# Linear attention and channel mix on one core: key moves on one queue, half of the weight loads behind unit 0's keys, other costs and due times in the plan

## The chip, the core and the metric

The kernel runs on one core of one Trainium2 chip. A core has a matrix engine (TensorE, PE in the profile) with its own sequencer for weight loads (PEld), two engines for elementwise work (VectorE or DVE, ScalarE or ACT), GpSimd (POOL) and SyncE (SP). SP and POOL issue the transfers of this kernel; the transfers themselves run on 16 DMA engines. The metric is the device time of one execution in microseconds, the median of the runs shown.

## The reference

A linear attention with a complex decay, followed by a channel mix. Per batch (4), head (8) and step (768), with a head size of 48:

```python
mag = np.sqrt(a_re * a_re + a_im * a_im)
scale = np.minimum(mag, 0.999) / (mag + 1e-06)
...
for t in range(S):
    new_re = ar * S_re - ai * S_im
    new_im = ar * S_im + ai * S_re
    kv = np.einsum('bhd,bhe->bhde', k[:, :, t], v[:, :, t])
    S_re, S_im = (new_re + kv, new_im)
    y[:, :, t] = np.einsum('bhd,bhde->bhe', q[:, :, t], S_re)
```

The heads are put side by side (x, 384 wide), and then, with x_prev the row before:

```python
xk = mu_k * x + (1.0 - mu_k) * x_prev
xr = mu_r * x + (1.0 - mu_r) * x_prev
k = np.maximum(xk @ w_k, 0.0)
v = k * k @ w_v
r = 1.0 / (1.0 + np.exp(-(xr @ w_r)))
return (r * v)
```

w_k is 384 x 1024, w_v 1024 x 384, w_r 384 x 384; everything is float32 (the weights arrive as 64-bit numbers and are converted on the chip).

## The kernel before

**Tiling.** The 4 x 768 rows are cut into eight units of 384 tokens (two halves per batch, the second one starting from the state of the first). Each unit has three steps:

- `gate(u)` loads a tile `g` of [a_re, a_im, k, q] in three parts of 128 channels (L662) and the values `v` (L671), and computes with ACT and DVE the decay's logarithm and angle, running sums of both, and at the end (`times`, L797, DVE) k and q multiplied by the cosine and by the sine of the angle.
- `attend(u)` is the attention. `stack(h)` moves a head's 48 channels of the cosine part and the 48 of the sine part of `g` into one tile `kq`, 112 rows high (L834, a transfer within the chip). Heads 2 and 5 straddle two parts of `g` and take two transfers for each part, so a unit has 20: heads with 48 rows move 144 KB at once. There are six buffers `kq` for eight heads, so the last two heads wait until the values of the first pairs are done; in unit 0 the last two use free space in `x0`. `scores` (sc, L914) multiplies keys and queries, DVE masks the result (pt, L923), `values` (y, L949 and L955) multiplies it with v and the state, ACT copies y to `ys` (L964), and ten transfers move `ys` into `xt` (L970), which is x with channels on partitions. `advance` carries the state: TensorE turns k (tr, L865), ACT copies it to `kt` (L871), and `up` (L885) multiplies it with v.
- `mix(u)` is the channel mix: differences and sums of x and x_prev on DVE and ACT, the products z (L461) for w_k and w_r, relu and square (L497, L501), the product with w_v (o, L528), and the store. For accuracy each float32 operand is split into a high and a low part (x and its rest, `hhi` and `hlo`), three products in place of one; unit 0 alone uses the whole float32 weights (L456, L525).

The weights come in ten pieces, `raw` (piece 0 of 384 KB, nine of 768 KB). `fetch(i)` loads a piece (`fetched`, L381), `convert(i)` makes float32 of it in three instructions on ACT and DVE (L589 to L599), and `split(i)` makes the high and the low part (L622, L625). Pieces 2 to 9 hold one block of w_k and one of w_v each. `look(i)`, 19 in all, loads a block of the weights once more (tile `again`, L638) and checks its range (DVE L642, ACT L644 and L645).

**What sets the order.** The whole program is a list of operations, each with its engine, its cost in us, what it reads and writes and which buffers it holds. The class `Plan` turns it into an order: each operation gets a due time, backwards from the products of TensorE, whose places come from the table `AT` (for each unit one pair of numbers for `attend` and one for `mix`); then a simulation of the engines starts, whenever an engine is free, the ready operation with the earliest due time. For SP and GP (POOL) it counts an issue time and a shared DMA stream with a START and an ARRIVE time. The instructions are emitted in the order of these simulated starts. So costs and due times change nothing but the order in which each engine's instructions stand (and, for operations that may run on either of two engines, which of them takes it). Between the times when `r` of unit 0's angle and its first hidden product are planned (FILL), an idle TensorE is given small products that nobody reads (`warm`, L1008, fillers).

`op_move` is an operation that either SP or POOL may issue; before the change all moves to kq and xt are of this kind. `op_dma` is one of SP, `op_dma_gp` one of POOL. Each engine works its instructions strictly in its own order, so a transfer that waits holds back those that stand behind it on the same engine.

## Time and profile before

| | us |
|---|---|
| median of three runs | 482.07 |
| lowest and highest | 478.08, 485.91 |
| the profiled execution, whole | 481.24 |
| its span in the trace | 479.5 |
| mean granted clock of TensorE | 0.958 |

The span is what the profile's page and its views divide by; 1.74 us of the profiled execution lie around it. What the page says of the transfers by number and queue, with the KB of each and the median us from issue to landing:

```profile
g<-in_gat SPq DMA_DIRECT2D x18, 768.0 KB, 6.0
kq<-g POOLq DMA_DIRECT2D x51, 144.0 KB, 5.5
again<-in_w_all SPq DMA_DIRECT2D x19, 384.0 KB, 4.1
kq<-g SPq DMA_DIRECT2D x43, 144.0 KB, 5.5
out_t<-zr SPq DMA_DIRECT2D x24, 192.0 KB, 2.0
```

The 144 KB moves of keys are split about evenly between the two queues. A wait in the views below is idle time of an engine and the event that ended it; it costs time only where that engine sets the end at that moment.

### The profile page before, as it was taken

The page shows a single profiled execution, that of the slowest core. Times are in us where ns is not written, and L with a number is a line of the kernel's source. Part 1 is how long each engine was busy: PE and PEld are TensorE (multiplying, and loading weights), DVE is VectorE, ACT ScalarE, POOL GpSimd, SP SyncE. Part 2 cuts the span into 40 slices and gives each one's busy share as a digit, 9 for nine tenths or more (in the row PEclk, how much of TensorE's full clock was granted, in tenths as well). Part 3 has the DMA queues.
Part 4 walks back from the last instruction along what each step waited for, and adds up shares of the span by engine and source line. Part 5 has one row for each costly group of instructions (what it writes and reads, how often), then busy time and mean ns, then how long its engine had stood idle before and what let it go on. Part 6 is the DMA issues. An engine that isn't in the chain of part 4 may idle for free.

```text
span 479.5 us, 9560 instructions
## 1 busy us (share of the span) xinstructions
PE 402.3 (84%) x3625; PEld 361.6 (75%) x3625; DVE 331.3 (69%) x523; ACT 346.1 (72%) x611; POOL 78.8 (16%) x179
## 2 busy tenths in 40 slices
PE   1015999999579997999799988999699979998994
PEld 1004985676368987989688977899588979898993
DVE  6794779477678996668777886696648985154322
ACT  5995558965769896979778896987686975335440
POOL 6332120211302120102110130202020020300000
PEclk9999799999889998999999998999689998999998
DMA  8999370708926671485947473597353182300101
GB/s 297 412 354 223 132 220 17 133 17 262 200 83 176 205 154 28 109 276 190 161 116 265 141 134 83 128 326 130 85 158 109 34 181 83 75 26 1 51 0 57
DMA packets 26053, 69.91 MB, mean 146 GB/s; under 512 B 5696, under 2 KB 10432, under 8 KB 26000
## 3 DMA queue, kind: packets, MB, share of 16 engines
q1 hardware_dynamic: 19232, 46.37, 33.9%
q0 software_dynamic: 6768, 22.86, 17.9%
q8 instruction: 30, 0.49, 0.4%
q14 instruction: 23, 0.19, 0.1%
HBM read 40.90 MB, written 4.72 MB: 95 GB/s over the span
## 4 chain that ended last, share of the span: by engine, by line
PE 36%; DMA 20%; issue 14%; ACT 13%; DVE 12%; POOL 3%; SPq 1%; POOLq 0%; DVEq 0%; ACTq 0%
PE z L461 11%; DMA kq<-g 11%; PE o L528 9%; PE sc L914 4%; DMA again<-in_w_all 4%; PE up L885 3%; DMA raw<-in_w_all 2%; DVE g L797 2%; DMA xt<-ys 2%; PE y L949 2%; PE o L525 2%; DVE ph L764 2%; PE y L955 2%; PE tr L865 1%; ACT r L303 1%
## 5 line engine op out<-in xcount | busy, mean ns | idle before, releaser
L461 PE MATMUL z<-x,w 128*128 128x384 f32 x693 | 132.0, 340 | 0.1
L461 PEld LDWEIGHTS z<-x,w 128*128 128x128 f32 x693 | 120.8, 188 | 2.2 <-issue 0.7
L528 PE MATMUL o<-hhi,w 128*128 128x384 f32 x336 | 89.0, 346 | 0.0
L834 POOL DMA_DIRECT2D kq<-g x77 | 39.0, 509 | 227.8 <-PE y L955 150.8
L914 PE MATMUL sc<-kq 112*64 112x64 f32 (+1 forms) x744 | 52.2, 283 | 25.2 <-DMA kq<-g 20.5
L914 PEld LDWEIGHTS sc<-kq 112*64 112x64 f32 x744 | 44.7, 159 | 35.0 <-issue 25.0
L528 PEld LDWEIGHTS o<-hhi,w 128*128 128x128 f32 x336 | 60.2, 190 | 2.1 <-issue 1.5
L528 PE MATMUL o<-hlo,w 128*128 128x384 f32 x168 | 57.3, 341 | 1.4 <-DVE hlo L509 1.4
L497 ACT ACTIVATE r<-z 128x384 f32<-128x384 f32 x64 | 31.0, 484 | 28.0 <-PE z L461 26.6
L865 PE MATMUL tr<-ident,g 128*128 128x128 f32 x120 | 22.0, 315 | 31.2 <-DVE g L797 31.2
L923 DVE TENSOR_TENSOR pt<-sc,masks 128x512 int32<-128x512 int32 x48 | 31.6, 684 | 23.8 <-PE sc L914 23.7
L797 DVE TENSOR_TENSOR g<-g,r 128x768 f32<-128x768 f32 x48 | 43.8, 951 | 4.2 <-ACT r L303 4.1
L865 PEld LDWEIGHTS tr<-ident,g 128*128 128x128 f32 x120 | 16.0, 160 | 34.7 <-DVE g L797 32.2
L970 POOL DMA_DIRECT2D xt<-ys x40 | 21.8, 546 | 91.5 <-ACT ys L964 84.6
L871 ACT COPY kt<-tr 128x384 f32<-128x384 f32 x40 | 18.1, 473 | 21.7 <-PE tr L865 21.5
L501 ACT ACTIVATE h<-r 128x384 f32<-128x384 f32 x64 | 33.0, 521 | 0.8
L528 PEld LDWEIGHTS o<-hlo,w 128*128 128x128 f32 x168 | 31.9, 190 | 1.7 <-DVE hlo L509 1.7
L885 PE MATMUL up<-v,kt 128*48 128x48 f32 (+1 forms) x640 | 25.5, 234 | 9.1 <-ACT kt L871 8.4
L885 PEld LDWEIGHTS up<-v,kt 128*48 128x48 f32 (+1 forms) x640 | 23.4, 145 | 12.2 <-ACT kt L871 11.2
L509 DVE TENSOR_TENSOR hlo<-h,hhi 128x384 fp32r<-128x384 f32 x56 | 30.9, 556 | 1.2
L319 DVE CAST hhi<-h 128x384 fp32r<-128x384 f32 x31 | 11.1, 357 | 29.0 <-PE o L528 17.3
L303 ACT ACTIVATE sq<-m 128x1152 f32<-128x1152 f32 (+2 forms) x27 | 27.7, 1049 | 3.6 <-DVE m L745 2.7
(91 smaller groups left out, 711.7 us busy)
## 6 DMA issues: line engine op xcount, KB each, us to landing
g<-in_gat SPq DMA_DIRECT2D x18, 768.0 KB, 6.0
kq<-g POOLq DMA_DIRECT2D x51, 144.0 KB, 5.5
again<-in_w_all SPq DMA_DIRECT2D x19, 384.0 KB, 4.1
raw<-in_w_all POOLq DMA_DIRECT2D x9, 768.0 KB, 10.8
kq<-g SPq DMA_DIRECT2D x43, 144.0 KB, 5.5
v<-in_vt SPq DMA_DIRECT2D x21, 288.0 KB, 5.1
out_t<-zr SPq DMA_DIRECT2D x24, 192.0 KB, 2.0
g<-in_gat SPq DMA_DIRECT2D x6, 384.0 KB, 4.7
```

Source lines behind the costliest of these rows:

```text
L303: nc.scalar.activation(out=out, in_=in_, func=func, **kw)
L461: nc.tensor.matmul(z, lhsT=wt[s[0]][:, part, s[1]], rhs=r[which][:, ct], start=n == 0, stop=n == 3 * NT - 1)
L497: nc.scalar.activation(out=t["r", j], in_=t["f", j], func=AF.Relu)
L501: nc.scalar.activation(out=t["h", j], in_=t["r", j], func=AF.Square)
L509: nc.vector.tensor_tensor(out=t["lo", j], in0=t["h", j], in1=t["hi", j].bitcast(F32), op=ALU.subtract)
L528: nc.tensor.matmul(tiles["o", mt], lhsT=wt[W_V + 2 * j][:, part, ts(mt, P)], rhs=r, start=j == 0 and n == 0, stop=j == NJ - 1 and n == 2)
L797: nc.vector.tensor_tensor(out=g[:, ct, 2 * i:2 * i + 2], in0=g[:, ct, 2:4], in1=t["r"][:, ct, 1 - i:2 - i].to_broadcast([P, 2, U]), op=ALU ...
L834: queue.dma_start(out=kq[h][i * HR + o:i * HR + o + n], in_=G[u][s, ct, 2 * i:2 * i + 2])
L865: nc.tensor.transpose(out=t["tr", c, part][:, ct * P:(ct + 1) * P], in_=G[u][:, ct, 2 * part, c * P:(c + 1) * P], identity=ident)
L885: nc.tensor.matmul(t["up", c][rows, h * D:(h + 1) * D], lhsT=both[:, cols], rhs=V[u][c][:, h * D:(h + 1) * D], start=True, stop=True)
L914: nc.tensor.matmul(sc[rows, i, cols], lhsT=kq[2 * p + j][:, 0, c * P + late * Q:][:, :Q], rhs=q if j else q[:, ::-1], start=True, stop=True)
L923: nc.vector.tensor_tensor(out=pts[k, c].bitcast(I32), in0=both, in1=masks.unsqueeze(1).to_broadcast([P, 2, 2, P]), op=ALU.bitwise_and)
```

## The change

- All moves to `kq` are issued by SP. The moves from `ys` to `xt` are also SP's, except in unit 0, where either engine may take them.
- Weight pieces 5 to 9 are loaded by SP, and only after all of unit 0's last products of the gate (its sine part, `kqs`) are there. Pieces 0 to 4 stay with POOL and no longer wait for a part of unit 0's gate.
- In the plan: another table `AT`; ARRIVE 1.3 for 0.9; a move is counted with 220 in place of 380 KB per ms; ACT and DVE instructions have 0.02 us more; the mask of the scores costs less; and the rule that a large transfer starts only when the stream is free now goes by a mark on each operation (`bulk`) instead of by its cost. Moves within the chip and the first two units' gate loads carry no such mark.

No instruction's work changes, only its place, and for the moves and half of the pieces the engine that issues them; the number of fillers, which the plan's idle times set, goes from 40 to 69. The lines of the changed kernel are those of before less one up to line 567, and one more from line 1008 on.

```diff
-AT = ((0.51, 1.23), (0.86, 1.42), (2.31, 2.4), (2.62, 3.27), (2.24, 2.87), (3.17, 4.12), (2.83, 3.65), (4.13, 5.17),
+AT = ((0.42, 0.67), (2.23, 4.26), (0.93, 2.49), (2.73, 3.06), (2.24, 2.87), (3.78, 4.38), (2.83, 3.48), (4.03, 5.22),
...
-FETCH_AT = 0
+FETCHED = 5
...
-    START, ARRIVE = 1.15, 0.9
-    BULK = 0.4
+    START, ARRIVE = 1.15, 1.3
...
-            if o["engine"] in self.QUEUE and o["cost"] > self.BULK and dma > t + self.START:
+            if o["bulk"] and dma > t + self.START:
                 return False
...
-        plan[0].op("ACT", 0.09 + n / 1200, f, **kw)
+        plan[0].op("ACT", 0.11 + n / 1200, f, **kw)
...
-        plan[0].op("DVE", 0.08 + n / (960 * rate), f, **kw)
+        plan[0].op("DVE", 0.1 + n / (960 * rate), f, **kw)
...
-        plan[0].op("SP", n / 380, f, **kw)
+        plan[0].op("SP", n / 380, f, **{"bulk": True, **kw})
...
-        plan[0].op("SP", n / 380, lambda e: f(nc.sync if e == "SP" else nc.gpsimd), other={"GP": n / 380}, **kw)
+        plan[0].op("SP", n / 220, lambda e: f(nc.sync if e == "SP" else nc.gpsimd), other={"GP": n / 220}, **kw)
...
-                raws[i] = fetched(keep, s, nc.gpsimd, tag=f"w{i}")[0]
-            op_dma_gp(393 * n, f, writes=[("raw", i)], reads=[("in", 0, FETCH_AT, 2)])
+                raws[i] = fetched(keep, s, nc.sync if i >= FETCHED else nc.gpsimd, tag=f"w{i}")[0]
+            late = i >= FETCHED
+            (op_dma if late else op_dma_gp)(393 * n, f, writes=[("raw", i)], reads=[("kqs", 0, ct) for ct in range(NT)] * late, bulk=late)
...
-                    uses=[g_slot[u]])
+                    uses=[g_slot[u]], bulk=u >= FIRST_LOAD)
...
-                        queue.dma_start(
+                        nc.sync.dma_start(
                             out=kq[h][i * HR + o:i * HR + o + n], in_=G[u][s, ct, 2 * i:2 * i + 2])
-                    op_move(n * 3.07, f, reads=[("kqs" if i else "kqc", u, r0 // P)], writes=[("st", u, h, i, r0)],
+                    plan[0].op("SP", n * 3.07 / 220, f, reads=[("kqs" if i else "kqc", u, r0 // P)], writes=[("st", u, h, i, r0)],
                            uses=[kq_slot[h], g_slot[u]])
...
-                op_dve(4 * P + 60, f1, reads=[("sc", u, k, c)], writes=[("pt", u, k, c)], uses=[sp, pt_slot[k, c]])
+                op_dve(4 * P, f1, reads=[("sc", u, k, c)], writes=[("pt", u, k, c)], uses=[sp, pt_slot[k, c]])
...
-                    op_move((src.stop - src.start) * 1.54, f, reads=[("ys", u, p), ("X0", u)], writes=[("Xp", u, i, dst.start)],
+                    k = (src.stop - src.start) * 1.54
+                    (op_move if u == 0 else lambda k, f, **kw: plan[0].op("SP", k / 220, lambda: f(nc.sync), **kw))(k, f, reads=[("ys", u, p), ("X0", u)], writes=[("Xp", u, i, dst.start)],
                            uses=[sy, x_slot[u]])
```

How it moves instructions shows in three places. The rows give line, operation, output<-input (with buffer numbers where names would read alike), shape, and a count.

SP at the start of the program, behind the loads of unit 0's gate (g_136): the moves of its keys. Before, seven of the moves into kq stand here with those into x0, the rest on POOL, and behind them comes the load of unit 2's gate (g_418):

```order
L834 DMA kq0_97<-g_136 48x768 x2
L834 DMA kq2_99<-g_136 48x768
L834 DMA kq4_101<-g_136 32x768
L834 DMA kq4_101<-g_136 16x768
L834 DMA kq2_99<-g_136 48x768
L834 DMA x0_132<-g_136 48x768
L834 DMA kq5_102<-g_136 48x768
L834 DMA x0_132<-g_136 16x768
L834 DMA x0_132<-g_136 32x768
L662 DMA g_418<-in_gat 128x1536 x2
```

After the change, from the third head on (six rows of kq0 to kq3 stand ahead of these):

```order
L834 DMA kq4_101<-g_136 32x768
L834 DMA kq2_99<-g_136 48x768
L834 DMA kq3_100<-g_136 48x768
L834 DMA kq4_101<-g_136 32x768
L834 DMA kq4_101<-g_136 16x768 x2
L834 DMA kq5_102<-g_136 48x768 x2
L834 DMA x0_132<-g_136 48x768 x2
L834 DMA x0_132<-g_136 16x768 x2
L834 DMA x0_132<-g_136 32x768 x2
L380 DMA raw_392<-in_w_all 128x6144
L380 DMA raw_413<-in_w_all 128x6144
```

All of unit 0's moves stand on SP, and two weight pieces follow them directly. POOL, which has the pieces, shows it from the other side. Before, with unit 1's gate g_150:

```order
L662 DMA g_150<-in_gat 128x768
L381 DMA raw_214<-in_w_all 128x6144
L381 DMA raw_223<-in_w_all 128x6144
L381 DMA raw_232<-in_w_all 128x6144
L834 DMA kq1_98<-g_136 48x768 x2
L381 DMA raw_249<-in_w_all 128x6144
L381 DMA raw_258<-in_w_all 128x3072
L834 DMA kq3_100<-g_136 48x768
```

After, with unit 1's gate g_140:

```order
L662 DMA g_140<-in_gat 128x768 x6
L671 DMA v_154<-in_vt 128x576
L671 DMA v_159<-in_vt 128x576
L671 DMA v_162<-in_vt 128x576
L380 DMA raw_165<-in_w_all 128x6144
L380 DMA raw_168<-in_w_all 128x6144
L380 DMA raw_173<-in_w_all 128x3072
L380 DMA raw_175<-in_w_all 128x6144
L380 DMA raw_179<-in_w_all 128x6144
L970 DMA xt_156<-ys_447 48x384
```

The last five pieces have left POOL, the first five stand behind the whole of unit 1's gate, and no keys stand among them.

TensorE where unit 4's first scores stand (unit 2's mix lies around them), before:

```order
L461 MATMUL z<-x,w 128x384 x9
L528 MATMUL o<-hhi,w 128x384 x2
L528 MATMUL o<-hlo,w 128x384
L528 MATMUL o<-hhi,w 128x384 x2
L528 MATMUL o<-hlo,w 128x384
L528 MATMUL o<-hhi,w 128x384 x2
L528 MATMUL o<-hlo,w 128x384
L865 MATMUL tr<-ident,g 128x128 x6
L914 MATMUL sc<-kq_97 64x128
```

After (three more products o and then the first score follow these rows):

```order
L460 MATMUL z<-x,w 128x384 x18
L865 MATMUL tr<-ident,g 128x128 x3
L527 MATMUL o<-hhi,w 128x384 x2
L527 MATMUL o<-hlo,w 128x384
L527 MATMUL o<-hhi,w 128x384 x2
L527 MATMUL o<-hlo,w 128x384
L527 MATMUL o<-hhi,w 128x384 x2
L527 MATMUL o<-hlo,w 128x384
L865 MATMUL tr<-ident,g 128x128 x3
L527 MATMUL o<-hhi,w 128x384 x2
L527 MATMUL o<-hlo,w 128x384
```

Between the first turn of the keys and the first score there are now 18 products o; before, there was none.

ACT in unit 6, around the copies to kt (kt_3451 before), before:

```order
L644 ACTIVATE again_3374<-again_3374,consts_82 128x384
L440 CAST x_3419<-xm_3242 128x384
L440 CAST x_3419<-xm_3391 128x384
L479 COPY zr_3423<-z_3397 128x384
L645 ACTIVATE again_3374,stat_92<-again_3374,consts_82 128x384
L440 CAST x_3344<-xm_3425 128x384
L871 COPY kt_3451<-tr_3428 128x8x48
L871 COPY kt_3451<-tr_3434 128x8x48
```

After (kt_3456 and kt_3518 are its first two chunks):

```order
L439 CAST x_3324<-xm_3432 128x384
L871 COPY kt_3456<-tr_3435 128x8x48
L871 COPY kt_3456<-tr_3441 128x8x48
L296 ACT_TABLE_LOAD
L302 ACTIVATE m_3305<-m_3305,consts_82 128x1152
L439 CAST x_3415<-xm_3492 128x384
L439 CAST x_3324<-xm_3503 128x384
L871 COPY kt_3518<-tr_3505 128x8x48
L871 COPY kt_3518<-tr_3511 128x8x48
L302 ACTIVATE ph_3306,stat_92<-m_3305 128x1152
L644 ACTIVATE again_3426<-again_3426,consts_82 128x384
```

The copies now stand ahead of the check's instruction (again, L644) and behind it no longer.

More of the change, by code (lines that the diff above doesn't have):

```diff
@@ L42 @@
 CAP = 0.999
-AT = ((0.51, 1.23), (0.86, 1.42), (2.31, 2.4), (2.62, 3.27), (2.24, 2.87), (3.17, 4.12), (2.83, 3.65), (4.13, 5.17),
-      (4.25, 4.38), (5.25, 6.43), (5.43, 5.51), (8.08, 8.34), (6.36, 7.7), (8.15, 11.01), (9.19, 9.24), (9.22, 10.06))
+AT = ((0.42, 0.67), (2.23, 4.26), (0.93, 2.49), (2.73, 3.06), (2.24, 2.87), (3.78, 4.38), (2.83, 3.48), (4.03, 5.22),
+      (3.96, 4.06), (5.16, 6.45), (5.4, 5.45), (9.16, 9.34), (6.35, 8.61), (9.06, 11.24), (9.26, 9.59), (9.6, 10.3))
 PAIRS = 0, 3, 1, 2
@@ L101, in op @@
     def op(self, engine, cost, emit, reads=(), writes=(), uses=(), table=None, heat=1.0, ahead=None, other=(),
-           kind=None):
+           kind=None, bulk=False):
         i, after = len(self.ops), set()
@@ L112, in op @@
         self.ops.append(dict(engine=engine, cost=cost, emit=emit, after=after - {None, i}, uses=uses, writes=writes,
-                             at=self.at, table=table, heat=heat, ahead=ahead, other=dict(other), kind=kind))
+                             at=self.at, table=table, heat=heat, ahead=ahead, other=dict(other), kind=kind, bulk=bulk))
     def steps(self, steps, a, b):
@@ L217, in run @@
                         ops.append(dict(engine=e, other={}, uses=(), table=None, heat=1.0, kind="full", cost=self.fill[0],
-                                        emit=self.fill[1], writes=(), after=()))
+                                        emit=self.fill[1], writes=(), after=(), bulk=False))
                         self.follow.append([])
@@ L307, in op_act @@
     def op_act(n, f, psum=False, **kw):
-        plan[0].op("ACT", 0.09 + n / 1200, f, **kw)
+        plan[0].op("ACT", 0.11 + n / 1200, f, **kw)
     def op_dve(n, f, rate=1, **kw):
-        plan[0].op("DVE", 0.08 + n / (960 * rate), f, **kw)
+        plan[0].op("DVE", 0.1 + n / (960 * rate), f, **kw)
     def op_dve_act(n, f, **kw):
         plan[0].op("DVE", 0.07 + n / 1920, lambda e: f(nc.scalar if e == "ACT" else nc.vector),
-                   other={"ACT": 0.09 + n / 1200}, **kw)
+                   other={"ACT": 0.11 + n / 1200}, **kw)
     def copy(engine, out, in_):
@@ L830, in move, with f @@
                 def move(r0, n, i):
-                    def f(queue):
+                    def f():
                         ct, o = r0 // P, r0 - h * D
                         s = slice(r0 - ct * P, r0 - ct * P + n)
-                        queue.dma_start(
+                        nc.sync.dma_start(
                             out=kq[h][i * HR + o:i * HR + o + n], in_=G[u][s, ct, 2 * i:2 * i + 2])
-                    op_move(n * 3.07, f, reads=[("kqs" if i else "kqc", u, r0 // P)], writes=[("st", u, h, i, r0)],
+                    plan[0].op("SP", n * 3.07 / 220, f, reads=[("kqs" if i else "kqc", u, r0 // P)], writes=[("st", u, h, i, r0)],
                            uses=[kq_slot[h], g_slot[u]])
```

## The prediction

> **What bounds the kernel now.** I read the page first (busy shares, slices), then the waits of each engine, then windows of 20 us for the granted clock, then the timeline around each wait of TensorE.
>
> ```profile
> PE 402.3 (84%) x3625; PEld 361.6 (75%) x3625; DVE 331.3 (69%) x523; ACT 346.1 (72%) x611; POOL 78.8 (16%) x179
> PE   1015999999579997999799988999699979998994
> PE sc L914 <- DMA kq<-g: 20.5, 18, 5.9
> PE up L885 <- ACT kt L871: 8.4, 6, 3.4
> POOL kq L834 <- PE y L955: 150.8, 8, 23.9
> ```
>
> TensorE is busy for 402.3 of 479.5 us. Its slices show two kinds of holes: the start (the first 48 us do little), and dips, one in nearly every unit. The waits (columns: sum in us, count, longest) say what ends the dips: a score product waiting for its stacked keys, 20.5 us in 18 waits, and `up` waiting for the copy of the turned keys, 8.4 us. POOL waits 150.8 us ahead of key moves for the last readers of a kq buffer; that is idle time of an issuing queue and costs nothing by itself.
>
> What the dips cost twice is in the windows (start:end, length, then PE, PEld, DVE, ACT, POOL busy, granted clock, DMA share, GB/s). After a dip the granted clock falls:
>
> ```profile
> 0.00:20.00 20.00, 1.65 (x6) 1.35 (x6) 13.08 (x20) 14.28 (x26) 11.51 (x40) 1.00 0.91 344
> 20.00:40.00 20.00, 5.41 (x27) 4.62 (x29) 19.63 (x27) 19.06 (x27) 5.81 (x11) 1.00 1.01 343
> 40.00:60.00 20.00, 14.09 (x226) 13.17 (x225) 10.76 (x16) 10.78 (x17) 2.93 (x6) 0.83 0.63 164
> 120.00:140.00 20.00, 13.44 (x147) 11.08 (x146) 13.48 (x23) 13.20 (x25) 3.79 (x8) 0.83 0.75 163
> 180.00:200.00 20.00, 17.74 (x178) 16.31 (x180) 12.52 (x22) 15.90 (x27) 0.00 (x0) 0.91 0.26 66
> 220.00:240.00 20.00, 17.14 (x129) 15.76 (x128) 14.42 (x24) 17.25 (x31) 4.39 (x9) 0.94 0.85 188
> 280.00:300.00 20.00, 16.39 (x144) 14.81 (x143) 15.04 (x27) 15.25 (x29) 2.52 (x5) 0.91 0.58 122
> 340.00:360.00 20.00, 17.47 (x231) 15.83 (x232) 12.45 (x23) 17.41 (x33) 2.98 (x6) 0.74 0.42 115
> 380.00:400.00 20.00, 17.42 (x141) 16.57 (x140) 16.32 (x29) 13.91 (x27) 3.51 (x7) 0.91 0.61 129
> ```
>
> After unit 1 the lost clock is (1 - clock) x 20: 3.4 + 1.8 + 1.2 + 1.8 + 5.2 + 1.8 = 15.2 us. The first two windows also say that the DMA engines are full there (0.91 and 1.01, 344 GB/s).
>
> **Part 1: the start (weights out of the way of unit 0's keys).**
>
> ```profile
> raw<-in_w_all POOLq DMA_DIRECT2D x9, 768.0 KB, 10.8
> g<-in_gat SPq DMA_DIRECT2D x6, 384.0 KB, 4.7
> v<-in_vt SPq DMA_DIRECT2D x21, 288.0 KB, 5.1
> x<-g POOLq DMA_DIRECT2D x1, 144.0 KB, 10.2
> x<-g SPq DMA_DIRECT2D x1, 144.0 KB, 10.4
> DMA to landing us min/median/max: 3.0/5.2/10.9
> 28.80 9.00 SPq L834 DMA_DIRECT2D kq<-g  x6
> 33.19 3.56 DVE L797 TENSOR_TENSOR g<-g,r 128x768 f32<-128x768 f32 x4
> 47.24 2.28 PE L914 MATMUL sc<-kq 112*64 112x128 f32 x24 [5.91 <-DMA kq<-g]
> 63.60 5.85 PE L1008 MATMUL warm<-ident 128*128 128x128 f32 x50
> 70.94 3.49 PE L456 MATMUL z<-x,raw 128*128 128x384 f32 x10 [0.84 <-DVE x L422]
> ```
>
> Unit 0's key moves (also into the two spare x0 slots) take about 10.3 us from issue to landing, against a median of 5.2 for all moves of keys, because 20.00:40.00 is full of weights. In the new order five pieces (384 + 4 x 768 KB), the two units' gates (12 x 384 KB) and values (3 x 288 KB) are ahead of the keys: 8928 KB or 9.1 MB, at 344 GB/s 27 us. So DMA is nearly empty when keys issue at 29 us and later. The last `times` ends at 33.19 + 3.56 = 36.8; I put it 0.7 us later, since the first piece now stands behind all of unit 1's gates, and ACT converts in front of the last sine (a choice between 0 and 2): 37.5. All 14 early moves now go by SP alone; the last that the first scores need leaves about two issues of 0.54 later, at 38.7 (0.54 us is the row of SP quoted in part 3), and lands between 3.0 and 5.2 us later: I take 3.6, so 42.3 in place of 47.24.
>
> From there to the first product took 70.94 - 0.84 - 47.24 = 22.9 us, with 3.4 us of it lost at clock 0.83. The new order has 28 more fillers (`warm`) in this stretch: 12 before and 16 after the values. A filler is two matmuls, 2 x 5.85 / 50 = 0.234 us, so 6.5 us. 22.9 - 3.4 + 6.5 = 26.0, first product at 68.3 instead of 70.1: -1.8 if the clock stays full, +1.6 if the 3.4 is lost again. I take **-1.5**. Five us won at the keys are mostly spent on fillers, which wait for the same x, itself behind values and moves.
>
> The other five pieces now leave on SP, behind those 14 moves; three of them also behind unit 0's xt moves. A piece takes 10.8 us, and its first product is that of the fourth hidden block at the earliest, some 20 us after 70. What covers them is that distance; without it each would cost up to 10.8. Unit 1's keys queue behind them on SP. Conversions move later with them, beside ACT and DVE that have 5 to 6 us in 20 free. I put 0 and keep +5 for the range.
>
> **Part 2: key waits of the later units.**
>
> ```profile
> 126.04 0.40 PE L914 MATMUL sc<-kq 112*64 112x128 f32 x2 [2.40 <-ACT kt L871]
> 129.60 0.92 PE L914 MATMUL sc<-kq 112*64 112x128 f32 x8 [3.16 <-DMA kq<-g]
> 181.47 1.31 PE L914 MATMUL sc<-kq 112*64 112x128 f32 x24 [1.81 <-DMA kq<-g]
> 235.29 0.40 PE L914 MATMUL sc<-kq 112*64 112x128 f32 x2 [1.48 <-DMA kq<-g]
> 236.44 0.55 PE L914 MATMUL sc<-kq 112*64 112x128 f32 x6 [0.74 <-DMA kq<-g]
> 287.09 0.88 PE L914 MATMUL sc<-kq 112*64 112x128 f32 x8 [2.10 <-issue]
> 394.88 1.39 PE L914 MATMUL sc<-kq 112*64 112x128 f32 x13 [2.00 <-DMA kq<-g]
> L528 PE MATMUL o<-hhi,w 128*128 128x384 f32 x336 | 89.0, 346 | 0.0
> ```
>
> These seven are units 2, 2, 3, 4, 4, 5 and 7 (the 2.10 marked as issue stands in front of scores of a kq too). In unit 4 the new order puts 18 `o` products between the first turn and the scores, where there were none: 18 x 0.346 = 6.2 us of work ready to run, so 2.22 becomes about 0.4. Unit 5 gets nine more in front (3.1 us): 2.10 becomes 0. Unit 2 gets six more native z rows ahead of its turn (12 matmuls of 0.35, 4.2 us): 5.56 becomes 2.5. Units 3 and 7 have no more in front than now. Sum: **-7.0**; ends 0 (the products are only moved, and the gap opens where they stood) and -13.7 (all gone).
>
> **Part 3: one queue in place of two.**
>
> ```profile
> L834 SPq DMA_DIRECT2D kq<-g x77: 503/543/1907, 28.8 to 413.2; - x77
> L970 POOL DMA_DIRECT2D xt<-ys x40 | 21.8, 546 | 91.5 <-ACT ys L964 84.6
> ```
>
> A move costs its queue 0.54 us (min/median/max in ns: 503/543/1907). Now the first eight keys of a pair go out one behind the other, 8 x 0.54 in place of 4 x 0.54: the last is 2.2 us late. Behind it on SP stand the other moves, the xt moves, and loads. Where products cover it (units 2, 4, 5) it costs nothing; in units 3, 6 and 7, 3 x 2.2 = **+6.5**. Ends: 0, and 7 x 2.2 = +15.4 with no cover anywhere. The 40 moves to xt that POOL issued (0.546 us each) join SP from unit 1 on, about five of the ten in a unit, each just after its ys; they meet key moves of the same unit's second half, and the products of the unit before lie beside them: 0, and up to +2 for the last unit, behind which no other unit stands. Nothing is saved on POOL that anybody waits for.
>
> **Part 4: `up` and the check of the weights.**
>
> ```profile
> 143.14 1.07 PE L885 MATMUL up<-v,kt 128*64 128x48 f32 x31 [2.18 <-ACT kt L871]
> 337.90 0.63 ACT L644 ACTIVATE again<-again,consts 128x384 f32<-128x384 uint8 x1 [4.74 <-DVE again L642]
> 341.56 1.83 PE L885 MATMUL up<-v,kt 128*64 128x48 f32 x31 [3.39 <-ACT kt L871]
> ```
>
> In unit 6 ACT stands 4.74 us in front of one `again`, and the copies to kt are behind it in the program: `up` waits 3.39. In the new order the copies of that place come before `again`: -3.4. In unit 2 scores now stand between turn and `up`: of 2.18 I take half, -1.1. Together **-4.5**, ends 0 (the wait is met elsewhere by another copy) and -8.4.
>
> **Part 5: the clock.** With the longest dips of units 2, 4, 5 and 6 gone, about half of 15.2 us of lost clock should go. A us at half clock costs only where TensorE is the one that sets the end; its share of busy time is 84%, not all of it on the path, so 0.6 of 7.8: **-4.7**, ends 0 and -12.
>
> Shorter costs in the plan for ACT, DVE and masks change no instruction; they act only by the order counted above.
>
> **Sum.** -1.5 - 7.0 + 6.5 - 4.5 - 4.7 = -11.2. Against the profiled execution, 481.24 us (span 479.5 and 1.74 around it): **470.0**. That execution lies 0.83 below the median of the runs shown, 482.07, so the forecast is 2.5% below the median. About 2% is what a measurement of this kernel can tell from no change: faster is below 472.4, slower above 491.7.
>
> **Rivals.**
> *Nothing gained (480).* For it: TensorE's own work is unchanged at about 402 us, fillers eat the start, and products moved in front of scores are missing later. Then parts 2 and 4 give -11.5 and get back as much in new waits; only -1.5 is left: 479.7. Against it: `again` and unit 4 have a plain cause.
> *Slower, by the one queue (495).* Each of seven units waits 2.2 us longer, plus a window's half clock of 1.7 after it: 7 x 3.9 = 27.3. The start and `up` still give 6.0 and half of part 2 3.5: 481.2 + 27.3 - 9.5 = 499.0, and 495.1 with one unit covered. It decides once five of the seven units have no cover (19.5 - 9.5 = +10). For it: eight landings in flight per queue and loads on SP in between; against it: the products that now stand in front of the scores of units 2, 4 and 5.
> *Keys slow for another reason (477).* The 10.3 us of unit 0's keys are the keys' own, or half the weights still run beside them. Then they land at 38.7 + 10.3 = 49.0, and 49.0 + 26.0 = 75.0 is 4.9 later than 70.1: +4.9 in place of -1.5, 476.4. The Trainium skill ("DMA: Bandwidth & Descriptors", section "Queues, rings and completion order") says that each DMA engine takes turns between the rows of different queues packet by packet; by that rule weights in POOL's queue would not hold up SP's keys, and taking them away wins nothing. The trace speaks against it as far as it goes: the x0 move by SP took 10.4 us, the one by POOL 10.2, with the weights in POOL's queue only.
> *Better (459).* All seven key waits and most lost clock go: -13.7 - 12 - 4.5 - 1.5 + 6.5 + 3 of waits that stay = 459.0.
>
> **How the numbers follow.** Forecast 470 (its own range 464 to 476): 0.42. Nothing gained: 0.26. Keys slow: 0.09. Better: 0.12. Slower: 0.11. The range 458 to 484 takes in all but the slower case and a part of the tails. Faster by over 2%: 0.12 + 0.34 of the forecast's 0.42 = 0.46. Slower by over 2%: 0.11. Within 2%: the rest, 0.43.
>
> **What would show it.** Part 1: unit 0's first scores at about 42, 41 fillers in a row, first product near 68. Part 2: no wait for keys over 1 us in units 4 and 5. Part 3: SP's key moves 0.54 us apart, and waits of 2 us in units 3, 6, 7. Part 4: no wait of `up` over 1 us in unit 6. Part 5: the clock at 1.00 in windows of units 4 to 6. What would make it wrong: new waits for converted weights in unit 0's products, or for keys in units whose order did not change.

## The result and the profile after

| | before | changed |
|---|---|---|
| median, us | 481.76 (4 runs, 478.08 to 485.91) | 431.94 (4 runs, 431.44 to 433.25) |
| profiled execution, us | 481.24 | 431.53 |
| span, us | 479.5 | 429.8 |
| mean granted clock | 0.958 | 0.996 |

The ratio is 0.899, 95% interval 0.894 to 0.905: faster by a tenth. The forecast was 470.0, its range 458 to 484; the time lies 26 us below the range. Executions more than 1.5% above the fastest of the same kernel, at a lower clock, are left out of the ratios and of the differences given below.

The page of the changed kernel, TensorE's busy time, its 40 slices and the clock in them:

```profile
PE 383.5 (89%) x3683; PEld 350.8 (82%) x3683; DVE 332.1 (77%) x528; ACT 340.7 (79%) x606; POOL 19.9 (5%) x59
PE   1006999999999999989999999999999999998993
PEclk9999999999999999999999999999999999999998
```

Once the start is over no slice up to the last few falls below 8 tenths, and the clock stays full until TensorE's last product at 423 us; the 1.7 us of lost clock left lie behind it. TensorE was idle for 479.5 - 402.3 = 77.2 us of the span before and is for 429.8 - 383.5 = 46.3 now: -30.9. Its busy time fell by 18.8, although it does the same products and 29 more fillers: that is mostly the clock. All other engines work as long as before (DVE 331.3 and 332.1, ACT 346.1 and 340.7), POOL apart, which gave its transfers away.

What TensorE still waits for, but for two waits of 0.3 and 0.2 us (engine, line, releaser; sum, count, longest):

```profile
PE tr L865 <- DVE g L797: 33.7, 3, 28.9
PE warm L1009 <- POOL consts L360: 1.7, 1, 1.7
PE o L527 <- DVE hlo L508: 1.7, 1, 1.7
PE z L460 <- ACT r L496: 1.0, 1, 1.0
PE up L885 <- ACT kt L871: 0.7, 1, 0.7
PE sc L914 <- DMA kq<-g: 0.4, 1, 0.4
```

32.5 of the 33.7 us are the start, which lies in front of everything; another 6.6 us of idle time lie behind TensorE's last product, as before. The 20.5 us of scores waiting for keys are 0.4, the 8.4 of `up` are 0.7.

Groups by line, scores and fillers of the kernel before (busy us, mean ns, idle in front):

```profile
L914 PE MATMUL sc<-kq 112*64 112x64 f32 (+1 forms) x744 | 52.2, 283 | 25.2 <-DMA kq<-g 20.5
L1008 PE MATMUL warm<-ident 128*128 128x128 f32 x80 | 12.8, 318 | 1.7 <-POOL consts L361 1.7
```

and the same of the changed kernel:

```profile
L914 PE MATMUL sc<-kq 112*64 112x128 f32 (+1 forms) x744 | 36.6, 250 | 0.5 <-DMA kq<-g 0.4
L1009 PE MATMUL warm<-ident 128*128 128x128 f32 x138 | 19.2, 300 | 1.7 <-POOL consts L360 1.7
```

The scores' 744 products took 52.2 us before with 25.2 of idle time in front of them, now 36.6 with 0.5. A product behind a wait not only starts late, it often ran at half clock too: 24 scores took 2.28 us at 47.24, where 48 take 2.23 now. In the trace before, 18.7 of the 52.2 us lie in stretches at half clock, which makes some 9 of the 15.6 us saved.

The lost clock is (1 - clock) x span: 20.1 us before, 1.7 now. Span less idle less lost clock is 382.2 before and 381.8 now, roughly TensorE's work at full clock. So by this account the 49.7 us are 30.9 of idle time and 18.4 of clock. The account is not exact. The lost clock also counts time at half clock in which TensorE is idle (7.8 of 40.4 us in the trace before), and the rest hides 6.4 us more of fillers (12.8 and 19.2) against about as much that the other products took less. They now stand in longer runs (35 waits of TensorE before, 10 now), and a short run costs more for each product: 2 scores took 0.40 us at 126.04, 48 in a row take 2.23. That this is the reason was not tested.

### The profile page after: what moved, and what is told of

Read it like the earlier page. It is cut to its first block, busy times and chain, and to the rows that moved or that the text cites. A ratio compares the mean times of both kernels' runs of the same rounds, so it can differ in the third digit from the quotient of the medians.

```text
span 429.8 us, 9500 instructions
## 1 busy us (share of the span) xinstructions
PE 383.5 (89%) x3683; PEld 350.8 (82%) x3683; DVE 332.1 (77%) x528; ACT 340.7 (79%) x606; POOL 19.9 (5%) x59
## 4 chain that ended last, share of the span: by engine, by line
PE 60%; DVE 13%; issue 10%; ACT 7%; DMA 7%; POOL 2%; SPq 0%; DVEq 0%; ACTq 0%; POOLq 0%
PE z L460 23%; PE o L527 15%; PE sc L914 4%; PE y L949 4%; PE z L455 4%; PE o L524 3%; PE y L955 3%; DMA g<-in_gat 2%; PE up L885 2%; DMA kq<-g 2%; ACT sq L302 2%; DVE g L797 1%; DVE ph L764 1%; PE tr L865 1%; DMA xt<-ys 1%
## 5 line engine op out<-in xcount | busy, mean ns | idle before, releaser
L527 PE MATMUL o<-hhi,w 128*128 128x384 f32 x336 | 87.5, 341 | 0.0
L865 PE MATMUL tr<-ident,g 128*128 128x128 f32 x120 | 19.2, 286 | 33.7 <-DVE g L797 33.7
L865 PEld LDWEIGHTS tr<-ident,g 128*128 128x128 f32 x120 | 14.2, 144 | 36.4 <-DVE g L797 34.7
L914 PEld LDWEIGHTS sc<-kq 112*64 112x64 f32 x744 | 33.5, 137 | 4.9 <-issue 2.5
L914 PE MATMUL sc<-kq 112*64 112x128 f32 (+1 forms) x744 | 36.6, 250 | 0.5 <-DMA kq<-g 0.4
L318 DVE CAST hhi<-h 128x384 fp32r<-128x384 f32 x34 | 12.2, 359 | 28.2 <-PE o L527 17.5
L442 DVE TENSOR_TENSOR x<-xm,x 128x384 fp32r<-128x384 f32 x42 | 22.7, 552 | 10.7 <-ACT x L439 10.6
L949 PE MATMUL y<-pt,v 128*48 128x128 f32 (+1 forms) x384 | 28.2, 277 | 0.2 <-DVE pt L923 0.2
L753 DVE TENSOR_TENSOR g<-g,sq 128x768 f32<-128x768 f32 x24 | 21.8, 952 | 5.4 <-ACT sq L302 5.2
L431 DVE SCALAR_TENSOR_TENSOR xm<-dx,mu_sb,xt 128x384 f32<-128x384 f32 x42 | 25.0, 614 | 0.8
```

Of the source, the lines that this page charges most:

```text
L527: nc.tensor.matmul(tiles["o", mt], lhsT=wt[W_V + 2 * j][:, part, ts(mt, P)], rhs=r, start=j == 0 and n == 0, stop=j == NJ - 1 and n == 2)
L865: nc.tensor.transpose(out=t["tr", c, part][:, ct * P:(ct + 1) * P], in_=G[u][:, ct, 2 * part, c * P:(c + 1) * P], identity=ident)
L914: nc.tensor.matmul(sc[rows, i, cols], lhsT=kq[2 * p + j][:, 0, c * P + late * Q:][:, :Q], rhs=q if j else q[:, ::-1], start=True, stop=True)
L949: nc.tensor.matmul(t["y", p][rows, ts(c, P)], lhsT=V[u][c][:, cols], rhs=w, start=c == 0, stop=False)
```

## The experiments

Each time is the median of its runs; the ratio is to runs of the kernel before on the same chip. The last three columns are of each run's profiled execution; the last is span less idle less lost clock.

| run | us | ratio (95% interval) | idle | lost clock | rest |
|---|---|---|---|---|---|
| kernel before | 481.76 | 1 | 77.2 | 20.1 | 382.2 |
| changed | 431.94 | 0.899 (0.894 to 0.905) | 46.3 | 1.7 | 381.8 |
| 1: changed order, two queues | 436.0 | 0.905 (0.894 to 0.915) | 49.8 | 2.2 | 383.5 |
| 2: order of before, SP alone | 485.56 | 1.003 (0.998 to 1.009) | 75.2 | 24.7 | 383.6 |
| 3: changed order, weights by POOL | 432.4 | 0.898 (0.887 to 0.909) | 46.6 | 2.1 | 381.2 |
| 9: changed order, all weights first | 434.15 | 0.904 (0.897 to 0.911) | 48.5 | 2.6 | 382.4 |
| 4: table and costs, old queues and weights | 472.32 | 0.981 (0.969 to 0.992) | 70.4 | 13.2 | 386.3 |
| 5: changed, old table | 464.44 | 0.965 (0.958 to 0.972) | 67.8 | 11.6 | 382.6 |
| 6: before, new table | 506.09 | 1.052 (1.042 to 1.063) | 86.4 | 24.5 | 389.9 |
| 7: changed, old costs | 466.78 | 0.969 (0.961 to 0.977) | 64.8 | 10.2 | 390.0 |
| 8: before, with fillers | 470.7 | 0.979 (0.968 to 0.990) | 60.3 | 7.0 | 400.9 |
| 10: changed, planned for two queues | 459.91 | 0.957 (0.950 to 0.964) | 66.1 | 7.8 | 386.8 |
| 11: changed, planned for early weights | 466.7 | 0.974 (0.967 to 0.980) | 64.2 | 12.1 | 388.2 |
| 13: changed, table moved, seed 1 | 466.52 | 0.961 (0.951 to 0.970) | 66.3 | 13.5 | 386.1 |
| 14: changed, table moved, seed 2 | 483.34 | 1.000 (0.995 to 1.004) | 74.8 | 25.7 | 385.0 |
| 15: before, table moved, seed 1 | 507.37 | 1.045 (1.035 to 1.055) | 96.9 | 29.5 | 381.8 |
| 16: before, table moved, seed 2 | 489.57 | 1.006 (1.001 to 1.011) | 85.1 | 22.0 | 382.1 |

Run 12 is told below. The rest is 381 to 390 in all rows but that with 21 us of fillers added: every order is in the main a matter of the two columns ahead of it. (The scatter does not follow the fillers that the plan puts in: runs 7 and 15 have 17.6 and 17.3 us of them, and 390.0 and 381.8 in the last column. Its cause is not shown.)

### One part at a fixed order (runs 1, 2, 3, 9)

In these, only the engine that issues a transfer differs; TensorE, ACT and DVE have the rows of the kernel they start from. Run 1, the sine half of the key moves on POOL again:

```diff
-                        nc.sync.dma_start(
+                        (nc.gpsimd if i else nc.sync).dma_start(
                             out=kq[h][i * HR + o:i * HR + o + n], in_=G[u][s, ct, 2 * i:2 * i + 2])
```

> The changed kernel with the sine half of each stacked-key move issued by POOL instead of SP; the order on TensorE, ACT and DVE is that of the changed kernel, row for row. Theory O (the order won it: more work stands ready in front of the scores, so keys may be some us late): within 1% of the changed kernel's 431.9, 428 to 437, waits of the scores for keys under 5 us in all. Theory Q (the queue won it: moves on POOL land late or block each other there): 445 or more, waits for keys back to 10 us or more and the median from issue to landing back from 3.5 to 5 us and over.

It took 436.0, 4.1 us more than the changed kernel, and its runs (435.64 to 437.37) do not touch those of the changed kernel. Its transfers, KB each and median us to landing:

```profile
kq<-g SPq DMA_DIRECT2D x47, 144.0 KB, 3.7
kq<-g POOLq DMA_DIRECT2D x47, 144.0 KB, 4.5
```

and its waits:

```profile
PE sc L914 <- DMA kq<-g: 3.7, 5, 1.0
```

Theory O holds: the order carries the gain, and the second queue costs some 4 us, 3.3 of them in waits for keys. (Only half of the moves to kq changed the queue here; those to xt stayed with SP.) The same rows of the changed kernel:

```profile
kq<-g SPq DMA_DIRECT2D x94, 144.0 KB, 3.5
L834 SPq DMA_DIRECT2D kq<-g x154: 503/580/1017, 32.3 to 361.0; - x154
```

A move costs SP 0.58 us to issue, nearly as forecast, but lands sooner than one of POOL.

Run 2 is the other side, the order of before with SP alone:

```diff
-                        queue.dma_start(
+                        nc.sync.dma_start(
                             out=kq[h][i * HR + o:i * HR + o + n], in_=G[u][s, ct, 2 * i:2 * i + 2])
...
-                        queue.dma_start(out=X[u][dst, i, 1:U + 1], in_=t["ys", p][src])
+                        (nc.sync if u else queue).dma_start(out=X[u][dst, i, 1:U + 1], in_=t["ys", p][src])
```

> The kernel before with every move to kq, and the moves to xt from unit 1 on, issued by SP, at the places the plan had given them; the order on TensorE, ACT and DVE is that of before. Theory O: 476 to 495, no gain, since the same work stands in front of the same scores; the forecast's 0.54 us for each move that joins SP would even add some us. Theory Q: 445 to 465, with the waits of the scores for keys (25 us idle in front of them before) cut by half or more.

485.56, no change. Its keys' transfers, then waits of TensorE:

```profile
kq<-g SPq DMA_DIRECT2D x94, 144.0 KB, 4.0
PE sc L914 <- DMA kq<-g: 15.1, 16, 4.8
PE sc L914 <- ACT kt L871: 4.0, 1, 4.0
PE y L949 <- DVE pt L923: 2.8, 6, 1.3
```

The median to landing fell from 5.5 to 4.0 us and the waits for keys from 20.5 to 15.1, yet the time did not fall. Other waits grew, those of the last two rows from 2.4 and 0.4, and TensorE's idle time is only 2.0 us lower. The clock is no reason: over the executions its mean is 0.955, as in those of the kernel before beside it; the profiled one, at 0.949, is low. The expected extra cost of SP's issues did not come either. The run is not about the queue alone: POOL, free of key moves, issued its last weight piece at 23.88 instead of 44.34.

Runs 3 and 9 put the late half of the weights on POOL and, in 9, ahead of unit 0's keys:

```diff
-                raws[i] = fetched(keep, s, nc.sync if i >= FETCHED else nc.gpsimd, tag=f"w{i}")[0]
+                raws[i] = fetched(keep, s, nc.gpsimd, tag=f"w{i}")[0]
```

> The changed kernel with weight pieces 5 to 9 issued by POOL directly behind pieces 0 to 4, so ahead of unit 0's keys, at unchanged order of the other engines. Theory W (full DMA engines held unit 0's keys): the keys of unit 0 take 8 us or more to land instead of 3.1, its first scores start at 46 to 49 instead of 42.6, and as much of that as the 41 fillers in front of the first product do not absorb ends up in the time: 433 to 438. Its rival (the keys were slow for their own reasons): first scores within 1 us of 42.6, time within 1 us of 431.9.

432.4, first scores at 42.3. But this run did not ask its question: of the five late pieces only two went ahead and had landed by 31.6, before the keys were issued at 32.3; three stood behind unit 0's moves to xt. Run 9 emits all ten behind one another:

```diff
-                raws[i] = fetched(keep, s, nc.sync if i >= FETCHED else nc.gpsimd, tag=f"w{i}")[0]
+                early = [i] if i < FETCHED - 1 else [*range(i, len(pieces))] if i < FETCHED else []
+                for k in early:
+                    raws[k] = fetched(keep, pieces[k], nc.gpsimd, tag=f"w{k}")[0]
```

> The changed kernel with all ten weight pieces issued by POOL one behind the other, ahead of unit 0's keys (in the earlier run with the weights on POOL only two of the five late pieces had gone ahead, and had landed before the keys were issued). Order of TensorE, ACT and DVE unchanged. Theory W (a full stream of weights holds unit 0's keys): they take 7 to 10 us to land instead of 3.1, the first scores wait until 45 to 48, and the time is 433 to 437, since the fillers behind can not give it all back at a fixed order. Rival: first scores within 1 us of 42.6 and 431.9 within 1.

434.15, on the timeline of TensorE:

```profile
41.63 0.55 PE L916 MATMUL sc<-kq 112*64 112x128 f32 x8
44.43 0.40 PE L916 MATMUL sc<-kq 112*64 112x128 f32 x2 [2.25 <-DMA kq<-g]
```

Unit 0's first four moves of keys now took 6.6 to 7.1 us to land instead of 3.1 to 3.4. Eight scores ran at 41.63, the others waited 2.25 us. Theory W is right in kind (weights in POOL's queue do hold the keys of SP's), and its price is near the bottom of what it expected: 2.2 us by the medians, with runs (432.22 to 435.43) that overlap those of the changed kernel, and 3.7 by the spans of the profiled executions. The Trainium skill ("DMA: Bandwidth & Descriptors", section "Queues, rings and completion order") has each DMA engine take turns between queues; 144 KB moves that take some 3.6 us longer beside 768 KB pieces of the other queue show that turns did not keep these small transfers fast.

### What the clock is worth (run 8)

The kernel before, with fillers in front of those products of units 2 to 7 that wait longest, for example in `scores`:

```diff
+                    for _ in range({2: 23, 3: 10, 4: 11, 5: 11, 7: 10}.get(u, 0) if k == c == 0 else 0):
+                        nc.tensor.matmul(sc[:, 0, :P], lhsT=ident, rhs=ident, start=True, stop=True)
```

> The kernel before with fillers (0.234 us each, overwritten by the product behind them) in front of the products of units 2 to 7 that wait longest: 23, 10, 11, 11 and 10 ahead of the first scores of units 2, 3, 4, 5 and 7, 3 and 9 ahead of the second and third up of unit 2, 14 ahead of the first up of unit 6. The waits' ends stay where they are; only the clock can change. Theory P (a us of lost clock is a us of time, since TensorE sets the end): the 15.2 us of lost clock behind unit 1 go to under 4, and the time falls by 10 to 15, to 467 to 472. The forecast's price (0.6 of it): 472 to 475 at the same clock. Rival (the clock is hidden behind other engines): 478 or more at a clock of 0.98.

470.7, 10.7 us below the kernel before beside it. Two of its windows (columns as in the prediction):

```profile
120.00:140.00 20.00, 18.69 (x207) 15.73 (x203) 15.17 (x25) 14.96 (x27) 4.54 (x9) 1.00 0.81 177
...
340.00:360.00 20.00, 18.57 (x230) 16.89 (x227) 15.12 (x26) 16.06 (x35) 4.01 (x8) 1.00 0.54 152
```

These two had a clock of 0.83 and 0.74; now it is full in both. The lost clock fell by 13.1 us, the span of the profiled execution by 11.3 and the time by 10.7, though the fillers do no work: 0.8 to 0.9 us of time for each us of lost clock. The fillers outlast the waits a little, which is in that price: idle time fell by 16.9 us and the last column of the table grew by 18.7. Theory P fits best and its rival (478 or more) falls, but the runs (468.53 to 475.29) scatter, and the interval of the ratio, 5 to 15 us, does not rule out the forecast's 0.6. The Trainium skill ("TensorE: Matmul & The Clock Gate", section "Part 1: The HAM clock gate") puts the cost of the ramp below 1% of a typical kernel's span; the kernel before lost 20.1 of 479.5 us, 4.2%, because its clock fell again behind the dips, in seven of its windows.

### Planning anew with one part exchanged (runs 4 to 7, 10, 11)

Here the order changes with the part. Run 4 leaves the moves to the plan again and fetches all weights early, so that table and costs are what stays of the change:

```diff
-FETCHED = 5
+FETCHED = 99
...
-                    plan[0].op("SP", n * 3.07 / 220, f, reads=[("kqs" if i else "kqc", u, r0 // P)], writes=[("st", u, h, i, r0)],
+                    op_move(n * 3.07, f, reads=[("kqs" if i else "kqc", u, r0 // P)], writes=[("st", u, h, i, r0)],
...
+                    op_move(k, f, reads=[("ys", u, p), ("X0", u)], writes=[("Xp", u, i, dst.start)],
```

> The changed kernel with the engine of the moves left to the plan again (SP or POOL) and all weight pieces loaded early by POOL: what stays of the change is the table of due times and the costs in the plan, and the order is planned anew from them. Theory O: 430 to 445, most of the gain is there. Theory Q: 460 to 480. The table was made for the other queues, so an odd unit with a new wait is possible under both: the waits for keys by unit tell.

472.32: waits of TensorE

```profile
PE up L885 <- ACT kt L871: 9.4, 7, 3.1
PE sc L914 <- DMA kq<-g: 6.0, 4, 3.1
```

Most of the waits for keys stay away, those of `up` are back. The time lies where Q put it, but not by Q's reason: at a fixed order the queues are worth 4 us (run 1) and the weights 2 (run 9), so it is mostly the new order, planned for other queues, that lost 40 us. Runs 5, 6 and 7 take the table and the costs apart (the values left out are those of the change's diff):

```diff
-AT = ((0.42, 0.67), (2.23, 4.26), (0.93, 2.49), (2.73, 3.06), (2.24, 2.87), (3.78, 4.38), (2.83, 3.48), (4.03, 5.22),
+AT = ((0.51, 1.23), (0.86, 1.42), (2.31, 2.4), (2.62, 3.27), (2.24, 2.87), (3.17, 4.12), (2.83, 3.65), (4.13, 5.17),
```

> The changed kernel with the table of due times of before; queues, weights and costs stay those of the change, and the order is planned anew. Theory T (the table is what put work in front of the scores): 460 or more, waits of TensorE back to 20 us outside the start. Theory C (the costs are: transfers counted longer, ACT and DVE dearer, so the plan starts moves earlier): 445 or less. Theory F (table, costs and queues fit only together, each exchanged alone loses most of the gain): 455 to 485.

464.44. The reverse, the new table in the kernel before:

> The kernel before with the new table of due times alone (old costs, moves on two queues, all pieces by POOL). Theory T: 465 or less. Theories C and F: 472 to 490; the last run with table and costs but the old queues took 472.3, and the costs are now missing too.

506.09, slower than the kernel before by 5% and outside the range of every theory, F's 472 to 490 too. And the old costs in the changed kernel:

```diff
-    START, ARRIVE = 1.15, 1.3
+    START, ARRIVE = 1.15, 0.9
...
-        plan[0].op("ACT", 0.11 + n / 1200, f, **kw)
+        plan[0].op("ACT", 0.09 + n / 1200, f, **kw)
...
-                    plan[0].op("SP", n * 3.07 / 220, f, reads=[("kqs" if i else "kqc", u, r0 // P)], writes=[("st", u, h, i, r0)],
+                    plan[0].op("SP", n * 3.07 / 380, f, reads=[("kqs" if i else "kqc", u, r0 // P)], writes=[("st", u, h, i, r0)],
```

> The changed kernel with the plan's costs of before (ARRIVE, the rate of moves, ACT, DVE, the mask); table, queues and weights stay those of the change. Theory C: 460 or more, with waits for keys or for kt of 15 us or more. Theory T: 445 or less. Theory F: 450 to 475.

466.78. Theories T and C fall, and F stands but for its miss in run 6: 32 to 35 us go whichever of the two is exchanged. Runs 10 and 11 do the same for run 4's two other parts, the queues (`op_move` as there, weights late) and the weights (`FETCHED = 99` alone):

> The changed kernel with the moves left to the plan (SP or POOL) and planned anew; the late half of the weights stays. With two queues and early weights together it took 472.3. Theory F (table, costs, queues and weights fit only together): 445 to 475. If only the weights' place mattered in that run: 437 or less here.

> The changed kernel with all pieces fetched by POOL as early as the plan likes, planned anew; all moves stay on SP. Theory F: 440 to 475. If only the queues mattered in the 472.3 run: 437 or less here.

459.91 and 466.7: again 28 and 35 us, for parts that are worth 4 and 2 at a fixed order.

### Is it the part, or any disturbance (runs 12 to 16)

If every exchange loses about as much, perhaps any change of the order does. Run 12 multiplied the whole table by 1.01:

> The changed kernel with every number of the table of due times 1% larger, planned anew, nothing else changed. Theory S (the order is one found by search, and the gain hangs on its exact fit, not on the table's shape): 440 to 470, with new waits and lost clock at places that the change had cleared. Theory R (the plan's rules give a good order over a stretch of due times): 429 to 437.

432.07, but the order was that of the changed kernel row for row: the table's numbers only rank the products of TensorE, and a common factor changes no rank. The run tells nothing of S or R; it is a repetition. So runs 13 to 16 moved each unit's pair by its own random amount up to 0.1, for example (seed 2):

```diff
-AT = ((0.42, 0.67), (2.23, 4.26), (0.93, 2.49), (2.73, 3.06), (2.24, 2.87), (3.78, 4.38), (2.83, 3.48), (4.03, 5.22),
+AT = ((0.51, 0.76), (2.32, 4.35), (0.84, 2.4), (2.65, 2.98), (2.31, 2.94), (3.83, 4.43), (2.86, 3.51), (3.99, 5.18),
```

> The changed kernel with each pair of the table moved by a random amount of at most 0.1 (first seed), planned anew; costs, queues and weights stay. Theory S (the gain hangs on the exact fit of a searched table): 450 to 475, as much lost as by exchanging table, costs or queues. Theory R (costs and queue make good orders, whatever the table's second decimal): 431 to 442.

> As the run before, with a second seed. Theory S: 450 to 475. Theory R: 431 to 442.

> The kernel before with its own table moved by the same random amounts (first seed). If its 481 is a searched fit too: 495 to 515, and the difference to the moved table of the changed kernel, some 30 to 45 us, is what costs, queue and weights are worth without the fit. If 481 is an ordinary order of these costs: 475 to 490.

> As the run before, with the second seed. Searched fit: 495 to 515. Ordinary order: 475 to 490.

466.52 and 483.34 on the side of the change, 507.37 and 489.57 on the other. The page and the waits of run 14:

```profile
PE 410.7 (85%) x3705; PEld 371.9 (77%) x3705; DVE 334.4 (69%) x523; ACT 347.8 (72%) x611; POOL 17.4 (4%) x59
PEclk9999799999998897899898898899979999999998
```

```profile
PE tr L865 <- DVE g L797: 41.7, 7, 31.2
PE up L885 <- ACT kt L871: 4.4, 4, 2.5
PE sc L914 <- DMA kq<-g: 3.8, 7, 1.5
PE o L527 <- DVE hhi L318: 3.7, 2, 2.8
```

With the changed kernel's queue, costs and weights, and a table moved by at most 0.1, the whole gain is gone, in a few short dips of every kind and the clock behind each of them. Theory S holds, though 483.34 lies above even its range: moving the table loses 35 and 51 us, no less than exchanging a part loses. So runs 5, 7, 10 and 11 can't show that a new cost or a queue is better; they could have lost as much if the old one were just as good. Moving the table of before by the same amounts lost 4.5% and 0.6% (23 and 3 us against the runs beside them); the first was expected of a searched fit, the second of an ordinary order. So it was less finely fitted, or had less to lose.

What stays open: what the new costs, the queue and the weights are worth without the fit. The moved tables differ by 41 us with one seed and by some 3 with the other (ratios 1.045 to 0.961, and 1.006 to 1.000), in favour of the change; two seeds do not settle it. It is also open whether a table as good could be found for the old costs.

## Why the prediction was wrong, point by point

**Part 1, the start: the size right, the reason in part.** The changed kernel's TensorE:

```profile
42.60 2.23 PE L914 MATMUL sc<-kq 112*64 112x128 f32 x48
...
58.63 9.42 PE L1009 MATMUL warm<-ident 128*128 128x128 f32 x82
67.89 5.97 PE L455 MATMUL z<-x,raw 128*128 128x384 f32 x18
```

Scores at 42.6 (forecast 42.3), 41 fillers of two matmuls in a row, first product at 67.9 (forecast 68.3; 30 more fillers lie between the two, where it counted 28). But no wait stands in front of the scores: the keys were there, and other products kept TensorE until 42.6. Nor was everything late before: eight scores ran from 40.72 on, and the first four key moves landed in 3.9 to 4.8 us; those behind them took 9.4 to 10.9, where they take 2.8 to 3.8 now.

That it was the weights, as argued, the runs bear out, and the queue had next to no part in it. Two queues without weights beside the keys (run 1, first row) start the scores at 42.8, SP alone with the weights early (run 2, second row) goes on with them at 46.95:

```profile
42.82 2.23 PE L914 MATMUL sc<-kq 112*64 112x128 f32 x48
...
46.95 2.55 PE L914 MATMUL sc<-kq 112*64 112x128 f32 x24 [4.80 <-DMA kq<-g]
```

How much the weights cost depends on how late they run: their last piece landed at 42.3 in run 2, and at 38.7 in run 9, where the wait ended at 44.4.

**Part 2, key waits: right in kind, far too small.** Forecast -7.0, priced on waits of 13.7 us; smaller ones of 5 us more were left out. The scores' waits fell from 20.5 to 0.4; less the start's 5.91 that is -14.2, and with the waits of 2.40 (kt) and 2.10 (issue) in front of scores, -18.7. Unit 4 did what the order showed:

```profile
207.78 0.49 PE L865 MATMUL tr<-ident,g 128*128 128x128 f32 x3
208.03 0.60 PE L527 MATMUL o<-hhi,w 128*128 128x384 f32 x2
...
209.68 0.49 PE L865 MATMUL tr<-ident,g 128*128 128x128 f32 x3
...
211.39 0.34 PE L527 MATMUL o<-hlo,w 128*128 128x384 f32 x1
211.66 2.23 PE L914 MATMUL sc<-kq 112*64 112x128 f32 x48
```

18 products between the first turn and the scores, and no wait. The step that failed is "Units 3 and 7 have no more in front than now": their waits went too, although in unit 7 the same rows stand in front of the scores (turn, nine products o, turn). The traces point to the keys. TensorE reached the scores 8.2 and 8.0 us behind the first key move of units 3 and 7, little more than before (7.2 and 7.7), but a move in those units landed in 2.2 to 4.5 us, where it took 3.1 to 7.6. With SP alone in the order of before (run 2) the waits for the first keys of these units had already fallen from 2.4 to 1.3 us each. I counted the work in front of the scores and not how soon the keys land.

**Part 3, one queue: wrong sign.** Forecast +6.5. The step that failed is "8 x 0.54 in place of 4 x 0.54: the last is 2.2 us late". The issue cost of 0.54 us was about right (0.58), but the sum took it as delay, with the landing times unchanged, and no such delay came. In the changed order two queues are 4.1 us slower than SP alone (run 1), in the order of before there is no difference (run 2). Moves land sooner from SP alone; that this more than makes up for the queueing is the likely reason, and is not shown apart. Parts 2 and 3 together were forecast at -0.5 and came to about -19.

**Part 4, `up`: right place, undersized.** Forecast -4.5; 8.4 to 0.7 is -7.7. The wait of 3.39 behind `again` in unit 6 is gone, and so are all others but one of 0.7; I had taken 3.9 us of them to stay.

**Part 5, the clock: undersized twice.** Forecast -4.7: half of 15.2 us goes, and each us is worth 0.6. All of it went (20.1 to 1.7 over the span, 3.4 of it in the start, where part 1 counted it), and run 8 puts a us at 0.8 to 0.9, though not clear of 0.6. The step that failed is "about half of 15.2 us of lost clock should go": only the longest dips were taken to go. With 15 us gone this term is off by about 8 us, and by 10 if a us of clock is a whole us of time. The four terms of parts 2 to 5 together make up most of the 38.5 us by which the profiled execution (431.53) lies below the forecast.

**The range.** Its lower end was the sum of the ends for single places, and still kept +6.5 for the queue and 3 us of waits. "Better (459)" was the right rival and 27 us short. The page allowed a better lower end: idle time outside the start (77.2 less the 38.9 up to the scores at 47.24) plus 20.1 of lost clock is 58 us, a span of 421. It is no strict bound, since an order can also win in the start, and nothing behind the last product. The changed kernel came to 429.8.

## What to carry to other kernels

- Where one engine bounds the kernel and its work is fixed, span = work + its idle time + its lost clock, here to within about 2%. When a whole order is searched anew, that sum gives the range's lower end; pricing the places where the order visibly differs finds only a part of it.
- To learn what a part of a planned kernel is worth, hold the order and change the part. Exchanging it in the planner's input measures the fit of a searched table (here 28 to 35 us for one part, and 35 and 51 for a mere move of the table), not the part (some 4 us for the queue, 2 to 4 for the weights).
- Fillers in the waits of an otherwise unchanged program tell what its lost clock is worth, and are themselves worth something when no better order is at hand (-10.7 us here).

## What the runs showed of the hardware

- Moves within the chip landed sooner when SP alone issued them: 144 KB in 3.5 us from SP alone, 3.7 and 4.5 from SP and POOL at the same order (run 1), and 4.0 against 5.5 and 5.5 at the order of before (run 2, where the weights went earlier too). Why is not shown.
- A dip costs clock beside the wait itself: 30.9 us of idle time and 18.4 of lost clock went together, 0.6 us of clock for each us of waiting.
- Loads of 768 KB in one queue slowed 144 KB moves of the other: unit 0's first four key moves took 6.6 to 7.1 us to land with such loads in flight (run 9), and 3.1 to 3.4 without.
